# A Fourier mixing layer and a feed-forward block on one core: two transform steps as whole fp32 matmuls, and half of the weights converted ahead of step D

## The chip, the core and the metric

The kernel runs on one core of one Trainium2 chip. The metric is device time in microseconds (us) for one execution, from the first to the last instruction of the core; smaller is better. Of the core's engines, TensorE (PE in the profile, its weight loads PEld), VectorE (DVE), ScalarE (ACT) and GpSimd (POOL) compute. SyncE (SP), ACT and POOL issue DMA transfers, which 16 DMA engines carry.

## The reference

```python
X = np.fft.rfft(x, axis=1)                     # x: (4, 3008, 256)
Xr, Xi = X.real, X.imag
Yr = Xr @ w_r - Xi @ w_i + b_r                 # w_r, w_i: (256, 256)
Yi = Xr @ w_i + Xi @ w_r + b_i
Yr = np.sign(Yr) * np.maximum(np.abs(Yr) - 0.01, 0.0)
Yi = np.sign(Yi) * np.maximum(np.abs(Yi) - 0.01, 0.0)
y = np.fft.irfft(Yr + 1j * Yi, n=3008, axis=1)
h = y.reshape(12032, 256) @ w_in               # w_in: (256, 2048)
g = np.maximum(h, 0.0) + alpha * np.minimum(h, 0.0)
return g @ w_out                               # w_out: (2048, 256)
```

All arrays are fp32.

## The kernel before

The Fourier transform of length 3008 = 47 x 64 is done as two matrix products each way. **Step A** (`a_mm`, L314) multiplies with a table of the 47-point transform, **step B** (`b_mm`) with the 64-point one and the twiddle factors, **step M** (`m_mm`, `m_evac`) mixes the channels and does the soft threshold, **step C** (`c_mm`, L466) and **step D** (`d_step`) go back. Then `l1_step` and `l2_step` are the two products of the feed-forward block. There are 4 batches. In steps A and C the unit of work is a group `g` of two rows (16 for a batch) and a pair `q` of frequency slots (12 for a batch).

Most products split each fp32 operand into two float32r (F32R) parts, `hi` (the upper bits) and `lo` (the rest), and add three matmuls: hi x hi, hi x lo, lo x hi. `split` (L124) makes `hi` by a copy on ACT or DVE and `lo` by a subtraction on DVE or POOL. Steps B and D are different: their operands stay F32, and each `PE.matmul` there is one whole fp32 matmul, which appears in the trace as two records.

The program is written out by hand in one order per engine. What comes before step D of batch 0, the *opening*, is:

1. 36 idle matmuls, then step A of all 16 groups of batch 0 and of the first 4 of batch 1 (`seq`), with splits three groups ahead; 3 idle matmuls follow each of the first 6 groups; then 40 idle matmuls.
2. A loop over `t` in 0 to 12, one pair per turn: `b_mm(t)`, the load for pair t+3, evacuations, `m_mm(t-1)`, `c_mm(t-3)`, and `pump(PT[t])`. A turn's second half waits for the table `rb_s`, of which slots 4 to 11 (pairs 2 to 5) are loaded after step A (`load_rb(4, 12)`).
3. The list `TAIL`, and `a_fill`: the last pairs' steps and the other 12 groups of step A of batch 1. Then step D of the first chunks.

`pump` does the conversion of the feed-forward weights, which arrive as 64-bit words: 16 pieces of 512 KB. A piece takes operations on ACT, four on DVE (`scalar_tensor_tensor` at L247 and three `tensor_scalar`), and three on POOL (L244, L250, L251; for some pieces L250 is on DVE). With one piece in work and the next begun, 4 pumps make a piece: n pieces take 4n + 3 pumps. `CL` (L203) is the number of pieces that are converted in the opening; the rest is pumped in the first 48 steps of the feed-forward block, `PAT[i]` pumps in step i. These 48 steps go in rounds of 6 (two blocks of 128 hidden columns, three chunks each).

`m_evac` (L419) of batch 0 does, on DVE, an add (L424), a clamp (L430) and a subtraction (L435), then ACT makes `Yh` (L440) and DVE `Yl` (L444, `m_evac2`). POOL issues the loads of `bt` (L345), negates two blocks for step M (`b_evac2`, L377) and loads the table `lc_s` of step C (L180).

Of the kernel before, what the change touches and what calls it, by code (L numbers as in the profile page):

```python
# [87 lines left out]

@with_exitstack
def fft_mix_moe(ctx, tc, x, w_r, w_i, b_r, b_i, w_in, w_out, alpha, la, rb, lc, rd, out):  # L90
    nc = tc.nc
# [208 lines left out]

    def a_split(b, g, e=None):
        t = xt[b, g // 2][:, 2 * (g % 2):2 * (g % 2) + 2]
        if b == 1 and g % 2 == 0 and g >= EARLY:
            hl = work.tile([NP, 4, C], F32R, tag="xt", name="xhl")
            hi, lo = hl[:, 0:2], hl[:, 2:4]
        else:
            th, tl = ("Xh", "Xl") if (b == 0 or g < EARLY) and g % 2 else ("xh", "xl")
            hi = work.tile([NP, 2, C], F32R, tag=th, name="xh")
            lo = work.tile([NP, 2, C], F32R, tag=tl, name="xl")
        split(t, hi, lo, e or A, G if g in (LG if b == 0 else LG1) and b < 2 else V)  # L310
# [321 lines left out]

    with tc.manual_schedule():
        nc.gpsimd.dma_start(out=la_s, in_=la)

# [13 lines left out]

        def start_split(n):  # L650
            for b, g in seq[n:n + 1]:
                a_split(b, g, A if g in (HA1 if b else HA) else V)

        for n in range(AHEAD):
            start_split(n)
# [173 lines left out]
```

## Time and profile before

| what | value |
|---|---|
| median of 3 runs (1426.1 to 1431.95) | 1427.29 us |
| the profiled execution, its own time | 1427.34 us |
| its span in the profile | 1425.6 us |
| mean granted TensorE clock | 0.987 of full |
| PE busy | 1387.9 us |
| DVE busy | 831.4 us |
| POOL busy | 440.3 us |

Times in the rows are us from the span's start. A granted clock of 1.00 is 2.4 GHz, 0.50 is 1.2 GHz. A busy PE isn't a PE at its peak: matmuls overlap, so one matmul's record is longer than the time by which it moves the next one on; the text takes that time from the starts.

### The profile page before, as it was taken

To read this page: it belongs to the slowest core of one execution; us is meant where nothing else is said; L and a number is where in the kernel's file an instruction comes from. 1 tells how busy PE (TensorE), PEld (TensorE's weight loads), DVE (VectorE), ACT (ScalarE), POOL (GpSimd) and SP (SyncE) were. 2 spreads that over 40 slices of the span, in tenths; PEclk is the share of its full clock that TensorE was granted. 3 is DMA by queue.
4 is the path that set the end of the run, shared out by engine and by line. 5 is a ranking of instruction groups with operands and counts; after the bars stand their busy time and mean duration, and the time that the engine had idled before them with its cause. 6 is when DMAs were issued, how large, how long until landed. Compare 5 with 4: busy or idle time off the path is not lost.

```text
span 1425.6 us, 25793 instructions
## 1 busy us (share of the span) xinstructions
PE 1387.9 (97%) x9990; PEld 1358.0 (95%) x9990; DVE 831.4 (58%) x1460; ACT 731.4 (51%) x1546; POOL 440.3 (31%) x506
## 2 busy tenths in 40 slices
PE   8979889999999999999999999999999999999998
PEld 5968879999999999999999999999999999999998
DVE  6896886666665444666666454565666444444443
ACT  4435555445445566454454566454544555555554
POOL 5763674222222222222222222222222222222221
PEclk8997999999999999999999999999999999999999
DMA  7954230111011232111110232111101000000000
GB/s 202 228 163 141 74 98 23 58 61 52 27 49 49 61 105 76 44 35 56 53 52 27 63 102 77 36 57 61 56 28 43 30 23 24 23 23 23 23 23 23
DMA packets 62710, 88.21 MB, mean 62 GB/s; under 512 B 10272, under 2 KB 45406, under 8 KB 62588
## 3 DMA queue, kind: packets, MB, share of 16 engines
q1 hardware_dynamic: 54668, 77.02, 18.1%
q0 software_dynamic: 4656, 6.40, 1.8%
q10 hardware_dynamic: 3264, 3.15, 0.6%
q8 instruction: 79, 1.29, 0.4%
q14 instruction: 43, 0.35, 0.1%
HBM read 49.02 MB, written 34.34 MB: 58 GB/s over the span
## 4 chain that ended last, share of the span: by engine, by line
PE 87%; DVE 6%; issue 2%; ACT 2%; DMA 2%; POOL 0%; SPq 0%; DVEq 0%; ACTq 0%; POOLq 0%
PE ps_h L535 35%; PE ps_o L584 8%; PE ps_o L582 8%; PE ps_o L583 8%; PE ps_m L411 5%; PE ps_d L519 4%; PE o_last L584 4%; PE o_last L583 4%; PE o_last L582 4%; PE ps_b L353 2%; PE ps_a L320 1%; PE ps_a L318 1%; PE ps_a L319 1%; DVE q L542 1%; DVE conv L247 1%
## 5 line engine op out<-in xcount | busy, mean ns | idle before, releaser
L535 PE MATMUL ps_h<-yh,w 128*128 128x384 f32 (+1 forms) x1984 | 584.9, 337 | 10.0 <-DVE q L542 10.0
L542 DVE SCALAR_TENSOR_TENSOR q<-q,beta_s,ps_h 128x384 f32<-128x384 f32 (+1 forms) x512 | 309.3, 604 | 346.6 <-ACT q L541 344.2
L547 POOL TENSOR_TENSOR gl<-q,gh 128x384 fp32r<-128x384 f32 (+1 forms) x252 | 257.9, 1023 | 795.8 <-ACT gh L546 678.7
L546 ACT ACTIVATE gh<-q 128x384 fp32r<-128x384 f32 (+1 forms) x512 | 265.8, 519 | 361.1 <-DVE q L542 358.2
L535 PEld LDWEIGHTS ps_h<-yh,w 128*128 128x128 f32 x1984 | 365.5, 188 | 15.3 <-DVE q L542 12.0
L535 PE MATMUL ps_h<-yl,w 128*128 128x384 f32 (+1 forms) x992 | 330.3, 333 | 0.0
L541 ACT ACTIVATE q<-ps_h 128x384 f32<-128x384 f32 (+1 forms) x512 | 245.5, 479 | 157.4 <-PE ps_h L535 140.9
L584 PE MATMUL ps_o<-w,gl 128*128 128x256 f32 x1024 | 289.5, 283 | 0.8 <-POOL gl L547 0.8
L582 PE MATMUL ps_o<-w,gh 128*128 128x256 f32 x1024 | 289.6, 283 | 0.0
L583 PE MATMUL ps_o<-w,gh 128*128 128x256 f32 x1024 | 285.1, 278 | 0.0
L547 DVE TENSOR_TENSOR gl<-q,gh 128x384 fp32r<-128x384 f32 (+1 forms) x260 | 157.0, 604 | 100.3 <-ACT gh L546 99.3
L584 PEld LDWEIGHTS ps_o<-w,gl 128*128 128x128 f32 x1024 | 192.9, 188 | 1.2 <-POOL gl L547 1.2
L583 PEld LDWEIGHTS ps_o<-w,gh 128*128 128x128 f32 x1024 | 192.8, 188 | 0.0
L582 PEld LDWEIGHTS ps_o<-w,gh 128*128 128x128 f32 x1024 | 192.7, 188 | 0.0
L535 PEld LDWEIGHTS ps_h<-yl,w 128*128 128x128 f32 x992 | 188.0, 190 | 1.3
L584 PE MATMUL o_last<-w,gl 128*128 128x256 f32 x480 | 135.3, 282 | 0.0
L583 PE MATMUL o_last<-w,gh 128*128 128x256 f32 x480 | 134.7, 281 | 0.0
L582 PE MATMUL o_last<-w,gh 128*128 128x256 f32 x480 | 134.2, 280 | 0.0
L584 PEld LDWEIGHTS o_last<-w,gl 128*128 128x128 f32 x480 | 90.7, 189 | 0.0
L582 PEld LDWEIGHTS o_last<-w,gh 128*128 128x128 f32 x480 | 90.3, 188 | 0.0
L583 PEld LDWEIGHTS o_last<-w,gh 128*128 128x128 f32 x480 | 90.2, 188 | 0.0
L519 PE MATMUL ps_d<-rd_s,zt 96*128 96x128 f32 x512 | 64.4, 281 | 0.0
(120 smaller groups left out, 1664.5 us busy)
## 6 DMA issues: line engine op xcount, KB each, us to landing
zt<-zd SPq DMA_DIRECT2D x32, 384.0 KB
ad<-ast SPq DMA_DIRECT2D x48, 192.0 KB
bt<-ad SPq DMA_DIRECT2D x72, 128.0 KB
zd<-zst SPq DMA_DIRECT2D x36, 256.0 KB
xt<-in_x SPq DMA_DIRECT2D x18, 320.0 KB
out<-os SPq DMA_DIRECT2D x34, 128.0 KB
x<-in_x SPq DMA_DIRECT2D x13, 320.0 KB
raw<-in_moe_w_in SPq DMA_DIRECT2D x8, 512.0 KB
```

Source lines behind the costliest of these rows:

```text
L247: lambda: V.scalar_tensor_tensor(out=v1, in0=wh, scalar=0xC0000000, in1=v1, op0=ALU.bitwise_and, op1=ALU.bitwise_or),
L353: PE.matmul(ps[:, s, ct], t[:, s, 128 * ct:128 * ct + 128], rb_s[:, 2 * q + s], start=True, stop=True)
L411: PE.matmul(p, a[:, k:k + 128], mix[i][:, w, ct], start=(n == 0), stop=(n == 3 * CT - 1))
L519: PE.matmul(ps[:, i], t[:, i, 128 * ct:128 * ct + 128], rd_s, start=True, stop=True)
L535: PE.matmul(ps, wi_h[m // FH][:, w, ct, 128 * (m % FH):128 * (m % FH) + 128], a[:, ct, 0:n], start=(k == 0), stop=(k == 3 * CT - 1))
L541: A.activation(out=q, in_=ps, func=AF.Relu, scale=-1.0)
L542: V.scalar_tensor_tensor(out=q, in0=q, scalar=beta_s[:, m:m + 1], in1=ps, op0=ALU.mult, op1=ALU.add)
L546: A.activation(out=hi, in_=q, func=AF.Copy)
L547: (V if LOS[(2 * m + c) % len(LOS)] and fill or not fill and (m + c) % 2 else G).tensor_tensor(out=lo, in0=q, in1=f(hi), op=ALU.subtract)
L582: PE.matmul(a, hi[:, t], w[:, 0], start=(i, k) in first, stop=False)
L583: PE.matmul(a, hi[:, t], w[:, 1], start=False, stop=False)
L584: PE.matmul(a, lo[:, t], w[:, 0], start=False, stop=(i, k) in last)
```

## The change

Step A of batches 0 and 1 takes `x` and a table `lf_s` in F32, one whole matmul for a group instead of three F32R ones, and its splits are gone, with the idle matmuls between the groups. In batch 0 DVE evacuates every second group. Step C of batch 0 takes the thresholded `Y` in F32 and a table `cf_s`: two whole matmuls for a pair instead of six, no `Yh` and no `Yl`. `cf_s` (half the bytes of `lc_s`) stands in the place of `lc_s`, which is loaded in step 26 of the feed-forward block, for batch 1. `CL` is 8, so 8 of 16 pieces are converted in the opening, and `PT` has 32 pumps instead of 19, with 3 left for `TAIL`. `PAT` is as it was.

```diff
@@ tables
+    cf_s = const.tile([128, NSLOT, 128], F32, tag="lc", name="cf_s")
+    def load_cf(n0, n1):
+        nc.gpsimd.dma_start(out=cf_s[:, n0:n1], in_=cf[:, n0:n1])
+    def load_lc():
+        lc_s = const.tile([128, 2, NSLOT, 128], F32R, tag="lc", name="lc_s")
...
+        for n in range(0, NSLOT, 6):
+            nc.gpsimd.dma_start(out=lc_s[:, :, n:n + 6], in_=lc[:, :, n:n + 6])
@@
-    CL = 4
+    CL = 8
@@ a_mm
+        if b < 2:
+            PE.matmul(ps, lf_s, xt[b, g // 2][:, 2 * (g % 2):2 * (g % 2) + 2], start=True, stop=True)
+            return
         hi, lo = xp.pop((b, g))
         PE.matmul(ps, la_s[:, 0], hi, start=True, stop=False)
         PE.matmul(ps, la_s[:, 1], hi, start=False, stop=False)
         PE.matmul(ps, la_s[:, 0], lo, start=False, stop=True)
@@ a_evac
-        A.activation(out=st, in_=ps, func=AF.Copy)
+        if b == 0 and g % 2:
+            V.tensor_copy(out=st, in_=ps)
+        else:
+            A.activation(out=st, in_=ps, func=AF.Copy)
@@ m_evac
-        m_less(b, q, t, c)
-        m_evac1(b, q)
+        y = work.tile([128, 2, C], F32, tag="Yh", name="Y")
+        V.tensor_tensor(out=y, in0=t, in1=c, op=ALU.subtract)
+        ys[b, q] = y
@@ c_mm
+        if b == 0:
+            y = ys.pop((b, q))
+            for s in range(2):
+                PE.matmul(ps[:, s], cf_s[:, 2 * q + s], y[:, s], start=True, stop=True)
+            return
@@
-    PT = [0, 0, 1, 2, 3, 2, 2, 1, 2, 3, 1, 2]
-    TAIL = [['s', 1, 1], ['p', 99], ['ce', 3], ['me', 1], ['s', 2, 0], ['cm', 2], ['m2', 1], ['f', 2], ['cm', 1], ['f', 0], ['ce', 2], ['ce', 1], ['f', 4]]
+    PT = [1, 2, 3, 3, 3, 3, 3, 3, 3, 3, 3, 2]
+    TAIL = [['ce', 3], ['me', 1], ['cm', 2], ['p', 99], ['f', 1], ['ce', 2], ['cm', 1], ['f', 1], ['ce', 1], ['f', 3]]
@@ opening
             a_mm(b, g)
-            if n < 6:
-                keep_warm(3)
@@ loop over t
-            run(m_evac2, t - 2)
-                load_lc(3 * t, 3 * t + 6)
+                load_cf(3 * t, 3 * t + 6)
-            if 9 <= t:
-                for g in range(2 * t - 18, 2 * t - 16):
-                    if EARLY // 2 <= g:
-                        a_load(1, g)
+            if 8 <= t < 11:
+                for g in range(2 * t - 14, 2 * t - 12):
+                    a_load(1, g)
@@ feed-forward block
+        at(LM, load_lc)
```

On **PE** the end of the opening (`TAIL` and `a_fill`) stands so before: the last step C in threes, then step A of batch 1 in threes, each third on a `lo` part (`xhl` and `xh`, `xl` are split parts of x).

```order
L473 MATMUL ps_c<-Yh,lc_s 128x256
L474 MATMUL ps_c<-Yh,lc_s 128x256
L475 MATMUL ps_c<-Yl,lc_s 128x256
L318 MATMUL ps_a<-xhl,la_s 96x512
L319 MATMUL ps_a<-xhl,la_s 96x512
L320 MATMUL ps_a<-xhl,la_s 96x512
L318 MATMUL ps_a<-xh,la_s 96x512
L319 MATMUL ps_a<-xh,la_s 96x512
L320 MATMUL ps_a<-xl,la_s 96x512
```

In the changed kernel (its own line numbers) the same place, up to step D:

```order
L486 MATMUL ps_c<-Y,cf_s 128x256 x4
L324 MATMUL ps_a<-x_292,lf_s 96x512
L486 MATMUL ps_c<-Y,cf_s 128x256 x2
L324 MATMUL ps_a<-x_292,lf_s 96x512 x11
L537 MATMUL ps_d<-rd_s,zt 128x128 x16
```

One group stands between the last two pairs of step C, and eleven groups follow without anything between them; before, two groups stood there and ten followed.

On **POOL** two turns of the loop (load of `bt`, the two negations, then conversion of a piece, `w` and `conv`) stand so before:

```order
L345 DMA bt<-a_82 128x1x256 x2
L377 TENSOR_SCALAR Xh<-Xh 128x4x64
L377 TENSOR_SCALAR Xl<-Xl 128x4x64
L244 TENSOR_TENSOR conv<-conv 128x512
L180 DMA lc_s<-tab_lc 128x2x768
L345 DMA bt<-a_82 128x1x256 x2
L377 TENSOR_SCALAR Xh<-Xh 128x4x64
L377 TENSOR_SCALAR Xl<-Xl 128x4x64
L250 TENSOR_TENSOR conv<-conv,w_385 128x512
L251 TENSOR_TENSOR w_385<-conv 128x2x256
```

and now:

```order
L356 DMA bt<-a_83 128x1x256 x2
L388 TENSOR_SCALAR Xh<-Xh 128x4x64
L388 TENSOR_SCALAR Xl<-Xl 128x4x64
L253 TENSOR_TENSOR conv<-conv 128x512
L259 TENSOR_TENSOR conv<-conv,w_243 128x512
L260 TENSOR_TENSOR w_243<-conv 128x2x256
L356 DMA bt<-a_83 128x1x256 x2
L388 TENSOR_SCALAR Xh<-Xh 128x4x64
L388 TENSOR_SCALAR Xl<-Xl 128x4x64
L253 TENSOR_TENSOR conv<-conv 128x512
```

A whole piece stands behind one pair, and the next piece begins behind the next.

On **DVE** one turn of the loop (threshold of one pair, `Xl` of another, conversion) stands so before:

```order
L424 TENSOR_TENSOR Yt<-ps_m,bias 128x512
L430 TENSOR_SCALAR Yc<-Yt 128x512
L435 TENSOR_TENSOR Yt<-Yt,Yc 128x512
L373 TENSOR_TENSOR Xl<-ps_b,Xh 128x4x128
L444 TENSOR_TENSOR Yl<-Yt,Yh 128x512
L235 TENSOR_SCALAR conv<-conv 128x512
L247 SCALAR_TENSOR_TENSOR conv<-raw,conv 128x512
```

and now:

```order
L435 TENSOR_TENSOR Yt<-ps_m,bias 128x512
L442 TENSOR_SCALAR Yc<-Yt 128x512
L438 TENSOR_TENSOR Y<-Yt,Yc 128x512
L384 TENSOR_TENSOR Xl<-ps_b,Xh 128x4x128
L244 TENSOR_SCALAR conv<-conv 128x512
L256 SCALAR_TENSOR_TENSOR conv<-raw,conv 128x512
L238 TENSOR_SCALAR conv<-conv 128x512
```

`Yl` is gone from the turn, and one more conversion operation stands in it.

## Rows read from the trace of the kernel before

**Rows 1.** The page's first part: busy us of each engine, share, instructions.
```profile
PE 1387.9 (97%) x9990; PEld 1358.0 (95%) x9990; DVE 831.4 (58%) x1460; ACT 731.4 (51%) x1546; POOL 440.3 (31%) x506
```
**Rows 2.** Busy by stretch: PE, PEld, DVE, ACT, POOL, granted clock, DMA share, GB/s.
```profile
57.00:98.00 41.00, 34.98 (x280) 33.31 (x278) 39.74 (x49) 16.04 (x28) 30.55 (x37) 1.00 0.71 204
105.70:118.36 12.66, 12.66 (x32) 8.33 (x31) 8.83 (x12) 6.98 (x12) 3.89 (x3) 0.50 0.74 232
```
**Rows 3.** PE in order of time, 0 to 45 us: start, us, instruction, idle time before.
```profile
4.84 0.71 PE L318 MATMUL ps_a<-xh,la_s 94*96 94x512 f32 x1
...
30.80 3.98 PE L631 MATMUL ps_idle<-idle 128*128 128x128 bf16 x40
...
42.10 1.13 PE L353 MATMUL ps_b<-rb_s,bt 128*128 128x128 f32 x8 [0.96 <-DMA rb_s<-tab_rb]
```
**Rows 4.** Stretches of step A, columns as in rows 2.
```profile
17.00:20.40 3.40, 2.65 (x11) 1.22 (x9) 3.30 (x5) 2.20 (x5) 1.80 (x3) 1.00 1.02 215
20.40:23.90 3.50, 2.22 (x9) 1.05 (x7) 3.40 (x4) 2.51 (x5) 2.74 (x2) 0.99 1.06 348
...
27.30:30.70 3.40, 3.40 (x9) 1.97 (x7) 1.44 (x1) 1.92 (x4) 3.40 (x5) 0.50 0.38 101
```
**Rows 5.** The chain that ended last, in order of time: start, us, what.
```profile
32.10 9.86 DMA rb_s<-tab_rb
...
118.57 3.43 PE ps_d L519 x16
```
**Rows 6.** DVE in order of time, in the loop and at its end.
```profile
71.07 2.83 DVE L444 TENSOR_TENSOR Yl<-Yt,Yh 128x512 fp32r<-128x512 f32 x1
...
75.97 0.43 DVE L430 TENSOR_SCALAR Yc<-Yt 128x512 f32<-128x512 f32 x1
76.43 0.69 DVE L435 TENSOR_TENSOR Yt<-Yt,Yc 128x512 f32<-128x512 f32 x1
...
77.82 0.93 DVE L444 TENSOR_TENSOR Yl<-Yt,Yh 128x512 fp32r<-128x512 f32 x1
78.68 0.68 DVE L247 SCALAR_TENSOR_TENSOR conv<-raw,conv 128x512 uint32<-128x512 uint32 x1
...
83.44 0.41 DVE L235 TENSOR_SCALAR conv<-conv 128x512 uint32<-128x512 uint32 x1
...
97.62 1.63 DVE L435 TENSOR_TENSOR Yt<-Yt,Yc 128x512 f32<-128x512 f32 x1
```
**Rows 7.** POOL in order of time, in the loop.
```profile
71.31 0.42 POOL L377 TENSOR_SCALAR Xh<-Xh 128x256 fp32r<-128x256 f32 x1
...
72.06 1.28 POOL L250 TENSOR_TENSOR conv<-conv,w 128x512 f32<-128x512 f32 x1
...
95.94 1.35 POOL L251 TENSOR_TENSOR w<-conv 128x512 fp32r<-128x512 f32 x1
```
**Rows 8.** Waits of PE, 122 to 240 us: us in total, times, longest.
```profile
PE ps_h L535 <- DVE q L542: 14.6, 20, 1.3
```
**Rows 9.** Rounds of 6 feed-forward steps, columns as in rows 2.
```profile
139.54:156.41 16.87, 13.33 (x90) 12.10 (x89) 15.66 (x21) 9.18 (x19) 11.65 (x9) 1.00 0.20 63
...
199.63:216.11 16.48, 11.85 (x77) 10.84 (x78) 15.22 (x20) 8.84 (x19) 11.97 (x9) 1.00 0.22 72
216.11:228.72 12.61, 11.31 (x84) 11.11 (x83) 10.46 (x17) 6.53 (x15) 8.30 (x7) 1.00 0.01 2
228.72:241.49 12.77, 12.77 (x96) 12.77 (x96) 6.78 (x15) 6.91 (x17) 3.66 (x5) 1.00 0.04 14
```
**Rows 10.** PE in order of time around step D (L519).
```profile
118.36 5.88 PE L519 MATMUL ps_d<-rd_s,zt 96*128 96x128 f32 x32
...
127.69 1.95 PE L519 MATMUL ps_d<-rd_s,zt 96*128 96x128 f32 x16
129.40 0.42 PE L535 MATMUL ps_h<-yh,w 128*128 128x384 f32 x1
```
**Rows 11.** POOL in order of time, in step A: the load of batch 1's x lands.
```profile
17.78 1.27 POOL L131 TENSOR_TENSOR xl<-x,xh 94x512 fp32r<-94x512 f32 x1 [0.50 <-DMA xt<-in_x]
```

More of the change, by code (lines that the diff above doesn't have):

```diff
@@ L84, in dft_tables, with fft_mix_moe @@
     f = np.float32
-    return (two_parts(la.astype(f)), rb.reshape(128, NSLOT, 128).astype(f),
-            two_parts(lc.reshape(128, NSLOT, 128).astype(f)), rd.astype(f))
+    la, lc = la.astype(f), lc.reshape(128, NSLOT, 128).astype(f)
+    return two_parts(la), rb.reshape(128, NSLOT, 128).astype(f), two_parts(lc), rd.astype(f), la, lc
 @with_exitstack
-def fft_mix_moe(ctx, tc, x, w_r, w_i, b_r, b_i, w_in, w_out, alpha, la, rb, lc, rd, out):
+def fft_mix_moe(ctx, tc, x, w_r, w_i, b_r, b_i, w_in, w_out, alpha, la, rb, lc, rd, lf, cf, out):
     nc = tc.nc
@@ L134, in fft_mix_moe @@
     la_s = const.tile([NP, 2, NQ], F32R, name="la_s")
+    lf_s = const.tile([NP, NQ], F32, name="lf_s")
     rb_s = const.tile([128, NSLOT, 128], F32, name="rb_s")
-    lc_s = const.tile([128, 2, NSLOT, 128], F32R, name="lc_s")
+    cf_s = const.tile([128, NSLOT, 128], F32, tag="lc", name="cf_s")
+    lc_h = []
     rd_s = const.tile([NQ, 128], F32, name="rd_s")
@@ L177, in load_rb @@
         nc.sync.dma_start(out=rb_s[:, n0:n1], in_=rb[:, n0:n1])
-    def load_lc(n0, n1):
-        nc.gpsimd.dma_start(out=lc_s[:, :, n0:n1], in_=lc[:, :, n0:n1])
+    def load_cf(n0, n1):
+        nc.gpsimd.dma_start(out=cf_s[:, n0:n1], in_=cf[:, n0:n1])
+    def load_lc():
+        lc_s = const.tile([128, 2, NSLOT, 128], F32R, tag="lc", name="lc_s")
+        lc_h.append(lc_s)
+        for n in range(0, NSLOT, 6):
+            nc.gpsimd.dma_start(out=lc_s[:, :, n:n + 6], in_=lc[:, :, n:n + 6])
     def split_mix():
@@ L299, in fft_mix_moe, with a_split @@
     xp = {}
-    def a_split(b, g, e=None):
+    def a_split(b, g):
         t = xt[b, g // 2][:, 2 * (g % 2):2 * (g % 2) + 2]
[L303 to L310, printed above, removed]
+        hi = work.tile([NP, 2, C], F32R, tag="xh", name="xh")
+        lo = work.tile([NP, 2, C], F32R, tag="xl", name="xl")
+        split(t, hi, lo, A, V)
         xp[b, g] = hi, lo
@@ L315, in a_mm @@
     def a_mm(b, g):
+        ps = ps_f.tile([NQ, 2, C], F32, tag="f", name="ps_a")
+        pa[b, g] = ps
+        if b < 2:
+            PE.matmul(ps, lf_s, xt[b, g // 2][:, 2 * (g % 2):2 * (g % 2) + 2], start=True, stop=True)
+            return
         hi, lo = xp.pop((b, g))
-        ps = ps_f.tile([NQ, 2, C], F32, tag="f", name="ps_a")
         PE.matmul(ps, la_s[:, 0], hi, start=True, stop=False)
@@ L320, in a_mm @@
         PE.matmul(ps, la_s[:, 0], lo, start=False, stop=True)
-        pa[b, g] = ps
     def a_evac(b, g):
@@ L468, in c_mm @@
             zd[b] = dram.tile([NQ, R, C], F32, tag="zd", name=f"zd{b}")
+        ps = ps_f.tile([128, 2, C], F32, tag="f", name="ps_c")
+        pc[b, q] = ps
+        if b == 0:
[3 more added lines that the diff above has]
+            return
         hi, lo, _ = ys.pop((b, q))
-        ps = ps_f.tile([128, 2, C], F32, tag="f", name="ps_c")
+        lc_s, = lc_h
         for s in range(2):
@@ L475, in c_mm @@
             PE.matmul(ps[:, s], lc_s[:, 0, k], lo[:, s], start=False, stop=True)
-        pc[b, q] = ps
     def c_evac(b, q):
@@ L633, in fft_mix_moe @@
     with tc.manual_schedule():
+        nc.gpsimd.dma_start(out=lf_s, in_=lf)
         nc.gpsimd.dma_start(out=la_s, in_=la)
@@ L648, in fft_mix_moe @@
         seq = [(0, g) for g in range(NG)] + [(1, g) for g in range(EARLY)]
[L650 to L655, printed above, removed]
         for n, (b, g) in enumerate(seq):
-            start_split(n + AHEAD)
             a_mm(b, g)
-            if n < 6:
-                keep_warm(3)
             if n >= 1:
@@ L682, in a_fill @@
             for g in range(a1[0], min(a1[0] + n, NG)):
-                if g + 3 < NG:
-                    a_split(1, g + 3, A if SE[(g + 3) % len(SE)] else V)
                 a_mm(1, g)
@@ L690, in fft_mix_moe @@
         for t in range(NPAIR + 1):
-            for g, e in AT.get(t, ()):
-                a_split(1, EARLY + g, A if e else V)
             run(b_mm, t)
@@ L706, in fft_mix_moe @@
             if t < 8 and t % 2 == 0:
-                load_lc(3 * t, 3 * t + 6)
-            if 9 <= t:
-                for g in range(2 * t - 18, 2 * t - 16):
-                    if EARLY // 2 <= g:
-                        a_load(1, g)
+                load_cf(3 * t, 3 * t + 6)
+            if 8 <= t < 11:
+                for g in range(2 * t - 14, 2 * t - 12):
+                    a_load(1, g)
         for op, *args in TAIL:
-            if op == "s":
-                a_split(1, EARLY + args[0], A if args[1] else V)
-            elif op == "f":
+            if op == "f":
                 a_fill(*args)
@@ L719, in fft_mix_moe @@
             else:
-                {"me": m_evac, "m2": m_evac2, "cm": c_mm, "ce": c_evac}[op](0, NPAIR - args[0])
+                {"me": m_evac, "cm": c_mm, "ce": c_evac}[op](0, NPAIR - args[0])
         put()
@@ L820 @@
         add(f"in_{name}", a)
-    for name, a in zip(("la", "rb", "lc", "rd"), dft_tables()):
+    for name, a in zip(("la", "rb", "lc", "rd", "lf", "cf"), dft_tables()):
         add(f"tab_{name}", a)
```

8 lines of the change are left out of this document (removed).

## The prediction

> **What bounds the kernel now.** I read the page's busy times first, then the busy times by stretch, then each stretch in order of time. PE is busy 1387.9 us of a span of 1425.6 [rows 1], so after the opening only work taken from PE, or idle time of PE, can bring anything. The opening (up to 124 us) and the first rounds of the feed-forward block (up to 229 us) are another matter.
>
> *Step A* begins on PE at 4.84 us and its last matmul makes way for the 40 idle ones at 30.80 [rows 3]. DVE is busy 3.30 of 3.40 us in its middle, with splits, while the granted clock is 1.00; PE then has gaps (2.22 of 3.50 us busy), and from the next row on the clock is 0.50, with PE busy without a gap [rows 4].
>
> *The gate of the loop* is a transfer: slots 4 to 11 of `rb_s` are asked for at 32.10, when step A has ended, and land 9.86 us later [rows 5]; `b_mm` of pair 2 starts at 42.10 behind it [rows 3].
>
> *The loop* ends for DVE with the last `m_evac`, at 97.62 + 1.63 = 99.25 [rows 6]: 57.2 us from the gate. DVE looks full (39.74 of 41.00 us, POOL 30.55) [rows 2], but much of it is waiting inside instructions. `Yl` takes 0.93 us at 77.82 and 2.83 us at 71.07 [rows 6]; the long one ends when POOL's row of 71.31 to 73.34 has run out [rows 6, 7]. So DVE operations that work from SBUF alone and POOL's tensor operations take turns. I call that the *shared turn* and add their undisturbed times:
>
> - a threshold: 0.43 + 0.69; a `Yl`: 0.93; a pair's two negations: 2 x 0.41 or 0.42 (0.82);
> - a piece: on DVE 0.68 + 3 x 0.41, on POOL 2 x 1.28 + 1.35, together 5.8 [rows 6, 7].
>
> From the gate on these are 12 thresholds (13.4), 11 `Yl` (10.2), 10 pairs of negations (8.2) and 4 pieces (23.3): 55.1 us, against 57.2 measured. The turn is taken all the time, and a stretch is 1.04 times the sum.
>
> *The end of the opening* runs from 99.25 to step D at 118.36 [rows 10], 19.1 us; for 12.66 us of it PE does step A of batch 1 without a gap at clock 0.50 [rows 2].
>
> *The first rounds*: PE waits 14.6 us for DVE's `q` [rows 8], which stands behind conversions. A round without conversion is 12.77 us less one step D, 1.71 from start to start [rows 9, 10]: 11.06. The six rounds from 139.54 to 228.72 take 89.2 [rows 9]; they hold 45 pumps (from the 7th to the 51st and last).
>
> **The change, part by part.** Durations are of one profiled execution, 1427.34 us by its own time, practically the median of the runs (1427.29).
>
> *A whole fp32 matmul.* Step D's are such: 16 records of 128 columns take 1.71 us from start to start at clock 1.00 (127.69 to 129.40) and 3.43 us at 0.50 [rows 10, 5], so 0.107 or 0.214 for 128 columns of one record. A group of step A has 512 columns and two records: 0.86 us at 2.4 GHz, 1.72 at 1.2.
>
> *Step A of the opening.* All splits go, and PE waits for x alone. The last x (batch 1's) has landed by 17.78 [rows 11]. I let two groups run at 1.2 GHz and 18 at 2.4: 4.84 + 3.44 + 15.5 = 23.8 instead of 30.8, **-7.0**. The gate follows its stores, so it moves by as much, to 35.1. The evacuations on ACT and DVE are shorter than a group. Both ends: 20 groups at 1.2 GHz give 39.2 (+8.4), all at 2.4 give 22.0 (-8.8).
>
> Which clock? At 1.00 PE kept it while it was busy 2.65 of 3.40 us with the same 94x96 operands, and lost it with 2.22 of 3.50 [rows 4]; now it has no gaps. At 0.50, though, step A without a gap didn't bring it back in 12.66 us [rows 2]; step D's whole fp32 matmuls did: 32 of them take 5.88 us, of which 16 took 3.43 [rows 10, 5]. I take 2.4 GHz, since stage and loop reach these groups at full clock. The Trainium skill (page "TensorE: Matmul & The Clock Gate", section "What's actually happening") says that the throttled clock is the default and that activity of TensorE releases it. By that rule groups without gaps come out at the sum below; the 12.66 us speak against it, and by them the first two rivals hold.
>
> *The loop.* `Yl` goes; the conversion grows from 19 to 32 pumps, of which 3 come before the gate; 29 / 4 = 7.25 pieces are 42.2 us. With thresholds (13.4) and negations (8.2) the sum is 63.8, times 1.04 is 66.2: **+9.0**. PE's share, with two whole matmuls of 256 columns (0.86 us) a pair for six split ones, stays covered: it was busy 34.98 of 41 us [rows 2] and the pairs now come more slowly. The tables are half as large, the raw pieces 2 MB more; the DMA share was 0.71 [rows 2]. In SP's queue the second load of `rb_s` (pairs 6 to 8) now stands behind a raw piece that waits for DVE in turn 2; with four turns until it is needed I cost that at nothing, and the loads of batch 1's x, moved forward to turns 8 to 10, too: no raw piece comes behind them before the block. Ends: nothing above the plain sum (-2.4), or DVE's PSUM operations, two of 0.68 us a pair by the same 512-element pattern as L247's row [rows 6], no longer hidden beside POOL in ten pairs (+13.6).
>
> *The end of the opening.* Behind the last threshold PE has two matmuls of step C (0.86), then 11 groups (9.5), which wait for no split; with 0.6 us for the handover 11.0 us instead of 19.1: **-8.1**. Three pumps are left over; they go to DVE, POOL and ACT beside these groups. `zt` is loaded meanwhile; SP has five stores ahead of it instead of six. At 1.2 GHz it is 20.4 (+1.3).
>
> *The first step D*: 32 records at 0.107 are 3.4 us instead of 5.6 (5.88 less the 0.3 by which the last record outlasts its turn): **-2.2**. With the clock down nothing is saved.
>
> *The first rounds.* 16 of the 51 pumps go. The six rounds exceed 6 x 11.06 = 66.4 by 22.8 us, 0.51 for a pump; some of it belongs to the combining of the mixing weights, which stays, so 0.45: **-7.2**. `PAT` gives 36 pumps by step 28, so the rounds 199.63 to 216.11 and 216.11 to 228.72 lose nearly all of theirs. The four loads of `lc_s` in step 26 stand in POOL's queue ahead of one conversion and the `gl` splits; two chunks wait in `gh` and `gl` (4 buffers each), so I cost them at nothing. Ends: 0, or 16 x 0.51 and the two rounds at 11.06 (-10).
>
> Sum: -7.0 + 9.0 - 8.1 - 2.2 - 7.2 = -15.5; 1427.3 - 15.5 = **1412 us**.
>
> **The rivals.**
>
> 1. *The clock is down at the end of the opening only.* For: the same place was at 0.50 before [rows 2]. Against: no gap now leads into it. Eleven groups cost 0.86 more (9.4) and step D's gain goes (2.2): 1423 us.
> 2. *Slower: the whole fp32 groups run at 1.2 GHz in both places.* Each costs 0.86 us more than I count. Eighteen more in the first stage (15.4) and rival 1's 11.6 make 1439 us. From 18 such groups on the change is a loss. For: the long stretch at 0.50 without a gap [rows 2, 4]. Against: step D's fp32 matmuls raised the clock [rows 10].
> 3. *The shared turn isn't filled so well*, since POOL's queue and DVE's now wait on each other for every piece, and the PSUM operations come on top: +13.6, 1425 us. For: POOL gets 1.6 times its work there. Against: the factor of 1.04 before.
> 4. *The first rounds don't shorten*, because `gl` splits fill the freed turn: +7.2, 1419 us. Against: the 11.06 us of the round without conversion.
>
> **How the numbers follow.** A measurement of this kernel can tell 0.5% (7.1 us) from no change. The forecast has 0.56, rival 4 0.10 (both faster by more than that), rival 1 0.12, rival 3 0.11 (both within it), rival 2 0.11 (slower). So 0.66 faster, 0.23 same, 0.11 slower. The range: down to 1403 (the loop at its plain sum, the rounds at -10, step A all at 2.4 GHz), up to 1426, which takes in rivals 1, 3 and 4 and leaves out rival 2 and a little at the bottom.
>
> **What would show it.** The idle matmuls behind step A begin near 24 us and the second `b_mm` stretch near 35; the last threshold ends near 101; step A of batch 1 is spaced by 0.86 us, with clock 1.00, and step D begins near 112; the rounds without conversion are two more than before, near 11 us each. A spacing of 1.72 us with clock 0.50 in step A, a last threshold after 110, or rounds that stay at 15 us would prove the forecast wrong.

## The result, and the profile after

| | median | runs | ratio to before, 95% interval |
|---|---|---|---|
| before | 1428.09 us | 4, 1426.1 to 1431.95 | |
| changed | 1413.49 us | 4, 1411.02 to 1415.04 | 0.9893 [0.9866, 0.9919] |

The change makes the kernel about 1% faster: the forecast was 1412 us. The profiled execution of the changed kernel took 1414.38 us by its own time, 13.0 less than that of before. The page's first part, which answers to [rows 1]:

```profile
PE 1381.0 (98%) x9916; PEld 1345.5 (95%) x9916; DVE 787.8 (56%) x1413; ACT 716.7 (51%) x1519; POOL 423.8 (30%) x497
```

PE is busy 6.9 us less by this row; the other 6 us are idle time that PE no longer has. Where they went stands in the order of time. PE of the changed kernel (start, us, instruction, idle time before it), to be read against [rows 3, 10]:

```profile
24.21 1.10 PE L324 MATMUL ps_a<-xt,lf_s 94*96 94x512 f32 x2 [1.43 <-ACT ast L342]
25.15 2.40 PE L641 MATMUL ps_idle<-idle 128*128 128x128 bf16 x40
...
36.56 1.13 PE L364 MATMUL ps_b<-rb_s,bt 128*128 128x128 f32 x8 [1.94 <-DMA rb_s<-tab_rb]
...
41.89 1.06 PE L364 MATMUL ps_b<-rb_s,bt 128*128 128x128 f32 x8
...
102.11 9.67 PE L324 MATMUL ps_a<-x,lf_s 94*96 94x512 f32 x22
112.36 3.90 PE L537 MATMUL ps_d<-rd_s,zt 96*128 96x128 f32 x32 [0.58 <-DMA zt<-zd]
```

Step A ends at 25.15 instead of 30.80, the gate (pair 2) opens at 36.56 instead of 42.10, and step D begins at 112.36 instead of 118.36. The 22 records before step D are 11 whole groups in 9.67 us, 0.87 apart: full clock. The granted clock by stretch, in step A, behind the gate and in that place (columns as in [rows 2]):

```profile
4.00:8.00 4.00, 4.00 (x15) 2.02 (x13) 0.21 (x1) 0.59 (x1) 0.00 (x0) 1.00 0.99 254
...
36.00:40.00 4.00, 3.44 (x20) 3.47 (x21) 2.12 (x4) 1.94 (x4) 1.99 (x3) 0.70 1.07 153
40.00:44.00 4.00, 4.00 (x32) 4.00 (x32) 2.69 (x6) 1.03 (x2) 3.15 (x6) 0.87 1.01 144
...
108.00:112.00 4.00, 3.78 (x9) 1.14 (x7) 0.00 (x0) 2.73 (x6) 0.00 (x0) 1.00 0.97 261
```

At the start of step A the row of the clock doesn't hold. The first group's records (count; duration in ns: least, median, most; first and last start) are

```profile
L324 PE MATMUL ps_a<-x,lf_s x2: 1061/1088/1114, 4.8 to 5.7; 94*96 94x512 f32 x2
```

and the median of step A's records is 592. So the first group, and part of the second, still ran at 1.2 GHz; from 7.2 us on the records of 592 ns show 2.4 GHz.

Behind PE's wait of 1.94 us at the gate the clock falls to 0.70 and 0.87, in PE-bound work: b_mm of the next pair comes 5.33 us behind the gate (3.77 to 3.84 in runs below where the clock held).

In the loop, the chain of waits (start, us, what) runs through the conversion: on POOL first, whose loads of `bt` stand behind it, then on DVE:

```profile
53.23 1.43 POOL conv L253
54.66 1.69 POOL conv L259
56.44 1.32 POOL w L260
58.33 1.37 POOL bt L356 x2
...
79.21 1.65 DVE conv L256
81.49 0.80 DVE Yc L442
```

Four of the seven rounds of the feed-forward block that answer to [rows 9], from the 7th step to the 49th:

```profile
132.51:147.60 15.09, 12.54 (x86) 11.52 (x85) 13.88 (x21) 8.59 (x19) 9.07 (x8) 1.00 0.23 69
...
175.55:190.46 14.91, 10.78 (x78) 10.38 (x77) 9.93 (x14) 5.74 (x13) 13.72 (x13) 1.00 0.33 101
190.46:203.45 12.99, 12.99 (x87) 12.99 (x87) 7.52 (x13) 6.82 (x14) 5.13 (x5) 0.87 0.36 129
203.45:214.77 11.32, 11.32 (x86) 11.32 (x85) 5.86 (x13) 5.67 (x12) 1.01 (x1) 1.00 0.00 0
```

They take 96.05 us in all (132.51 to 228.56), against 101.95 before. PE's wait for `q` halved, and another grew from 0.8 us before (118 to 242 us), both in the waits from 112 to 229 us (total, times, longest):

```profile
PE ps_h L553 <- DVE q L560: 7.1, 9, 1.5
PE ps_o L602 <- POOL gl L565: 5.3, 4, 2.6
```

All stages of the profiled executions, this one's and those of the experiments below, stand in one table. "Loop" is from the gate to the end of the last threshold (pair 11), "end" from there to step D, "first steps" from step D to DVE's 7th `q`, "rounds" from the 7th to the 49th; what follows is 1184 us in each (1183.8 to 1184.4).

| kernel | gate at | loop | end | first steps | rounds | span |
|---|---|---|---|---|---|---|
| before | 42.10 | 60.70 | 15.56 | 21.18 | 101.95 | 1425.6 |
| changed | 36.56 | 64.46 | 11.34 | 20.15 | 96.05 | 1412.6 |
| a_only | 36.81 | 58.99 | 12.71 | 21.23 | 101.26 | 1415.3 |
| c_only | 45.42 | 52.75 | 13.06 | 21.11 | 102.04 | 1418.2 |
| b_cl8 | 44.75 | 74.24 | 15.36 | 19.55 | 91.76 | 1429.7 |
| cl4 | 36.27 | 50.51 | 11.27 | 20.65 | 102.10 | 1404.8 |
| lc_late | 34.50 | 63.13 | 11.96 | 20.99 | 91.74 | 1406.7 |
| cl5_tail | 37.26 | 52.91 | 11.73 | 20.34 | 100.64 | 1406.9 |
| best | 36.60 | 50.86 | 11.65 | 22.75 | 99.83 | 1406.0 |
| best_warm | 36.76 | 50.82 | 11.45 | 21.01 | 99.90 | 1404.2 |
| no_warm | 48.41 | 62.99 | 11.27 | 19.76 | 96.06 | 1422.5 |

### The profile page after: what moved, and what is told of

It reads as the page before. It is cut to its first block, busy times and chain, and to the rows that moved or that the text cites. A ratio compares the mean times of both kernels' runs of the same rounds, so it can differ in the third digit from the quotient of the medians.

```text
span 1412.6 us, 25487 instructions
## 1 busy us (share of the span) xinstructions
PE 1381.0 (98%) x9916; PEld 1345.5 (95%) x9916; DVE 787.8 (56%) x1413; ACT 716.7 (51%) x1519; POOL 423.8 (30%) x497
## 4 chain that ended last, share of the span: by engine, by line
PE 87%; DVE 3%; POOL 3%; DMA 3%; issue 2%; ACT 1%; SPq 1%; ACTq 0%; DVEq 0%; POOLq 0%
PE ps_h L553 35%; PE ps_o L602 8%; PE ps_o L600 8%; PE ps_o L601 8%; PE ps_m L422 5%; PE o_last L602 4%; PE o_last L601 4%; PE o_last L600 4%; PE ps_d L537 4%; PE ps_b L364 2%; DMA x<-in_x 1%; DVE conv L256 1%; PE ps_m L408 1%; DVE q L560 1%; DMA raw<-in_moe_w_in 1%
## 5 line engine op out<-in xcount | busy, mean ns | idle before, releaser
L565 DVE TENSOR_TENSOR gl<-q,gh 128x384 fp32r<-128x384 f32 (+1 forms) x260 | 152.3, 586 | 103.9 <-ACT gh L564 101.8
```

Source lines behind the costliest of these rows:

```text
L565: (V if LOS[(2 * m + c) % len(LOS)] and fill or not fill and (m + c) % 2 else G).tensor_tensor(out=lo, in0=q, in1=f(hi), op=ALU.subtract)
```

## The experiments

The theory to be tested: the whole fp32 steps are the gain, and converting four more pieces ahead takes back part of it, since in the loop DVE and POOL share the turn in which the pieces are made. The rival: the work moved ahead is what pays.

### The parts apart

**The whole fp32 steps without the moved pieces** (cl4):

```diff
-    CL = 8
+    CL = 4
-    PT = [1, 2, 3, 3, 3, 3, 3, 3, 3, 3, 3, 2]
+    PT = [0, 0, 1, 2, 3, 2, 2, 1, 2, 3, 1, 2]
```

> The changed kernel with CL = 4 and the PT of before: 19 pumps in the opening instead of 35, the two transform steps stay whole fp32. Theory (shared turn): the four pieces that are put back into the first feed-forward rounds cost about 5.9 us there (the six rounds from 132.51 to 228.56 took 96.05, those of before 101.95) and took 5.8 us each of the turn of DVE and POOL in the loop. Without them PE bounds the loop at 46 to 49 us from the gate instead of 64.5, step D begins near 97 instead of 112.4, the rounds take near 102: 1404 us, between 1400 and 1408. Rival (converting ahead is what pays): the rounds give back more than the loop wins, 1420 us or more. Rival (the loop is bound by something else, such as DVE's PSUM operations or the transfers): the loop stays above 58 us and the time at 1411 to 1418.

Measured: 1406.56 us (5 runs, 1405.36 to 1408.11), ratio to before 0.9849 [0.9828, 0.987]. This lies in the theory's range (1400 to 1408), and both rivals fall. Its loop as one stretch, and PE's rows there:

```profile
36.27:86.78 50.51, 50.51 (x389) 49.08 (x390) 43.04 (x62) 18.90 (x32) 38.29 (x49) 1.00 0.72 202
```

```profile
40.11 1.08 PE L364 MATMUL ps_b<-rb_s,bt 128*128 128x128 f32 x8
44.75 1.05 PE L364 MATMUL ps_b<-rb_s,bt 128*128 128x128 f32 x8
49.38 1.05 PE L364 MATMUL ps_b<-rb_s,bt 128*128 128x128 f32 x8
```

PE is busy in all 50.51 us, 4.63 us a pair: the loop is PE's own. The changed kernel's loop is 13.95 us longer by the four pieces, and its rounds 6.05 shorter.

**The moved pieces without the whole fp32 steps** (b_cl8: the kernel before, with)

```diff
-    CL = 4
+    CL = 8
-    PT = [0, 0, 1, 2, 3, 2, 2, 1, 2, 3, 1, 2]
+    PT = [1, 2, 3, 3, 3, 3, 3, 3, 3, 3, 3, 2]
-    TAIL = [['s', 1, 1], ['p', 99], ['ce', 3], ['me', 1], ['s', 2, 0], ['cm', 2], ['m2', 1], ['f', 2], ['cm', 1], ['f', 0], ['ce', 2], ['ce', 1], ['f', 4]]
+    TAIL = [['p', 99], ['s', 1, 1], ['ce', 3], ['me', 1], ['s', 2, 0], ['cm', 2], ['m2', 1], ['f', 2], ['cm', 1], ['f', 0], ['ce', 2], ['ce', 1], ['f', 4]]
```

> The kernel before with the second part of the change alone: CL = 8, the PT of the changed kernel, and the remaining pumps first in TAIL; steps A and C stay split. Theory (shared turn): thresholds 13.4, Yl 10.2, negations 8.2 and 7.25 pieces 42.2 us sum to 74.0, times 1.04 is 77 us for the loop against 57.2, and the six feed-forward rounds give back 6 to 7: about 1441 us, between 1435 and 1448. Rival (converting ahead pays by itself): 1420 us or less.

Measured: 1432.97 us (12 runs, 1429.84 to 1435.94), ratio 1.0034 [1.0022, 1.0047]: slower than before, as the theory has it, though by less than its range (1435 to 1448). The loop grew by 13.54 us (60.70 to 74.24) and the rounds gave back 10.19, where 6 to 7 were forecast. The gate came 2.65 us later, which is not from the edit: step A ahead of it is the same program, but in this execution it ended at 33.82 instead of 30.80, with a clock of 0.50 from 10 us on against a mean of 0.75 before. Two of its rounds:

```profile
196.95:209.61 12.66, 11.43 (x85) 11.23 (x84) 8.97 (x13) 5.63 (x13) 11.07 (x9) 1.00 0.02 6
209.61:221.12 11.51, 11.51 (x88) 11.51 (x87) 7.27 (x14) 6.26 (x14) 4.63 (x4) 1.00 0.00 1
```

The same two rounds of the changed kernel took 14.91 and 12.99. This kernel loads `lc_s` in its opening; the changed one does so in step 26, in the first of the two. That led to lc_late below.

**Step A alone as whole fp32** (a_only; the kernel before, with)

```diff
+        if b < 2:
+            pa[b, g] = ps
+            PE.matmul(ps, lf_s, xt[b, g // 2][:, 2 * (g % 2):2 * (g % 2) + 2], start=True, stop=True)
+            return
...
-            if n < 6:
-                keep_warm(3)
```

> The kernel before with step A of batches 0 and 1 alone as whole fp32 matmuls; step C stays split and CL is 4. Theory: the gate of the loop comes 5.5 us earlier, the end of the opening (last threshold to step D) takes 11 to 12 us instead of 19.1 at a granted clock of 1.00, the first step D takes 2 us less, the loop stays at 57 us and the rounds at 102: -15 us, 1412 us, between 1409 and 1416. Rival (the clock at the end of the opening needs the whole fp32 matmuls of step C as well): it stays at 0.50 there, groups of step A 1.72 us apart, 1423 us.

Measured: 1416.46 us (6 runs, 1415.76 to 1417.72), ratio 0.9917 [0.9901, 0.9934], just above the expected range (1409 to 1416). The groups at the end of the opening ran at full clock (20 records in 8.75 us), so the rival falls. But PE then waited 1.93 us for `zt`, and the clock fell in step D, whose 32 records took 7.07 us instead of the changed kernel's 3.90. In order of time:

```profile
97.83 8.75 PE L315 MATMUL ps_a<-x,lf_s 94*96 94x512 f32 x20
108.51 7.07 PE L522 MATMUL ps_d<-rd_s,zt 96*128 96x128 f32 x32 [1.93 <-DMA zt<-zd]
```

**Step C alone as whole fp32** (c_only; the kernel before, with)

```diff
-        m_less(b, q, t, c)
-        m_evac1(b, q)
+        y = work.tile([128, 2, C], F32, tag="Yh", name="Y")
+        V.tensor_tensor(out=y, in0=t, in1=c, op=ALU.subtract)
+        ys[b, q] = y
```

and `c_mm`, `load_cf` and `load_lc` as in the change.

> The kernel before with step C of batch 0 alone as whole fp32 matmuls (no Yh, no Yl; lc_s loaded in the feed-forward block); step A stays split and CL is 4. Theory: Yl (10.2 us of the shared turn) goes, PE bounds the loop at 48 to 50 us instead of 57.2; step A of batch 1 keeps its splits and its clock of 0.50, so the end of the opening stays near 19 us: about -8, 1419 us, between 1416 and 1423. Rival (the last step C as whole fp32 raises the clock for what follows): the end of the opening takes 12 to 14 us and the time is 1412 to 1414. Rival (Yl was hidden in waits): 1426 to 1429.

Measured: 1418.5 us (6 runs, 1415.52 to 1420.09), ratio 0.9928 [0.9909, 0.9947]: in the theory's range. The loop fell from 60.70 to 52.75 us. Of those 52.75 some 1.4 are again a clock that fell behind the gate, after a wait of 2.90 us: the next b_mm came 5.21 us later. Two things that the theory didn't have nearly cancel in this execution. The gate came 3.32 us later, as its split step A ran at 0.50 and ended at 33.69. And the end took 13.06 us instead of 15.56, since the clock stayed up for longer than before, where it is 0.50 from 105.70 on, 2.9 us behind the last threshold [rows 2]:

```profile
98.17:106.40 8.23, 6.55 (x25) 3.42 (x24) 8.06 (x11) 4.92 (x10) 5.56 (x4) 1.00 0.69 220
106.40:111.23 4.83, 4.83 (x13) 2.92 (x12) 2.69 (x6) 3.12 (x6) 0.00 (x0) 0.50 0.94 293
```

The second rival named such an end, 12 to 14 us. But the clock did fall again in it, and step C can't have raised a clock that was full already; why it stayed up for longer is open.

By the medians of this set of runs (before 1428.77) step A brings 12.3 us, step C 10.3, and both together 22.2 (cl4). The parts add up. The moved pieces cost 4.2 on the kernel before, and 6.9 on the whole fp32 steps (1413.49 against 1406.56; the first is from the set of the result, where before took 1428.09).

### Whether two engines share a turn

The theory's turn was read from pairs of long rows. This run has neither transform nor block, only DVE and POOL operations on 128x512 tiles:

```diff
+    for kind in ("two", "one", "psum"):
+        stage(kind, 12, 0)
+    stage("two", 0, 12)
+    for kind, nv in (("two", 24), ("one", 40), ("psum", 24)):
+        stage(kind, nv, 12)
```

> No transform and no feed-forward block: the output is zeros. In separate stages DVE does 128x512 fp32 operations by themselves (tensor_tensor from SBUF, tensor_scalar from SBUF, tensor_tensor with one operand from PSUM), POOL does tensor_tensor by itself, and then each kind of DVE operation runs beside 12 of POOL's. Theory (shared turn): alone 0.69, 0.43, 0.68 and 1.28 us as in the loop; beside POOL, 24 two-operand DVE operations (16.6) and 12 of POOL's (15.4) take about 32 us, 40 tensor_scalar (17) and 12 of POOL's also about 32, but the 24 from PSUM overlap and take 17 to 20. Rival (no turn is shared, the long Yl rows were something else): all three stages take 16 to 18 us.

Measured, in order of time: DVE alone with two operands from SBUF, with one, and with one from PSUM; POOL alone; then POOL beside each of the three.

```profile
22.94 8.69 DVE L120 TENSOR_TENSOR vo<-va,vb 128x512 f32<-128x512 f32 x12
...
34.74 4.57 DVE L122 TENSOR_SCALAR vo<-va 128x512 f32<-128x512 f32 x10
...
42.20 8.67 DVE L124 TENSOR_TENSOR vo<-ps,vb 128x512 f32<-128x512 f32 x12
...
53.07 16.50 POOL L126 TENSOR_TENSOR go<-ga,gb 128x512 f32<-128x512 f32 x12
...
71.72 20.11 POOL L126 TENSOR_TENSOR go<-ga,gb 128x512 f32<-128x512 f32 x12
72.40 28.70 DVE L120 TENSOR_TENSOR vo<-va,vb 128x512 f32<-128x512 f32 x24
...
103.55 16.99 POOL L126 TENSOR_TENSOR go<-ga,gb 128x512 f32<-128x512 f32 x12
...
105.34 27.94 DVE L122 TENSOR_SCALAR vo<-va 128x512 f32<-128x512 f32 x38
...
135.50 16.55 POOL L126 TENSOR_TENSOR go<-ga,gb 128x512 f32<-128x512 f32 x12
136.18 17.37 DVE L124 TENSOR_TENSOR vo<-ps,vb 128x512 f32<-128x512 f32 x24
```

Beside POOL, 24 two-operand operations take 28.70 us instead of 17.4 (twice 8.69), 38 of one operand 27.94 instead of 17.4; with an operand in PSUM DVE is as fast as alone. So the turn is shared, and only by operations from SBUF: the rival falls. The Trainium skill (page "GPSIMD Engine Reference", section "Specifications") says that GpSimd's SBUF interfaces are shared with VectorE, for two SBUF inputs or a two-port mode. The rows of two operands and of PSUM agree; in which mode the operations of one operand ran, no run shows.

But the times don't add up as the theory has it (32 us). Records from the stretch of two operands in which both engines work, and of POOL alone:

```profile
L120 DVE TENSOR_TENSOR vo<-va,vb x11: 1632/1633/1636, 72.4 to 89.1; 128x512 f32<-128x512 f32 x11
L126 POOL TENSOR_TENSOR go<-ga,gb x10: 1588/1590/1591, 73.6 to 88.6; 128x512 f32<-128x512 f32 x10
L126 POOL TENSOR_TENSOR go<-ga,gb x11: 1259/1262/1262, 54.9 to 68.3; 128x512 f32<-128x512 f32 x11
```

The two engines start operations alternately, one and one, each 1.67 us apart (72.4 to 89.1 in ten steps). Alone, DVE's are 0.73 apart and POOL's 1.34. So a pair of operations takes 1.67 us where the sum is 2.07, a factor of 0.81; with one operand it takes 1.40 of 1.80, a factor of 0.78.

### The wait that the change brings

`lc_s` later (lc_late; the changed kernel, with)

```diff
-        for n in range(0, NSLOT, 6):
-            nc.gpsimd.dma_start(out=lc_s[:, :, n:n + 6], in_=lc[:, :, n:n + 6])
+        for k in range(4):
+            at(42 + 2 * k, load_lc_part, 6 * k)
```

> The changed kernel with the four loads of lc_s one each in steps 42, 44, 46 and 48 of the feed-forward block instead of all in step 26. Theory (the four issues hold up POOL's queue for 2.94 us, and the third term of ps_o waits 2.6 us for a gl behind them): the rounds from the 7th step to the 49th take 93 to 94 us instead of 96.05, the time is 1411 us, between 1410 and 1412. Rival (another gl split is late there all the same, as in the kernel before with CL = 8 alone, which loads lc_s in the opening and has one wait of 2.0 us for gl): within 1 us of 1413.5.

Measured: 1408.8 us (5 runs, 1406.55 to 1409.65), ratio 0.9867 [0.9844, 0.9891]. The theory's sign, and more than its size: the rounds take 91.74 us, 4.3 less, as b_cl8's did. The changed kernel's POOL around the loads with PE's wait behind it, then two of lc_late's rounds:

```profile
182.94 1.61 POOL L259 TENSOR_TENSOR conv<-conv,w 128x512 f32<-128x512 f32 x1
184.50 2.94 POOL L189 DMA_DIRECT2D lc_s<-tab_lc  x4
187.47 1.27 POOL L260 TENSOR_TENSOR w<-conv 128x512 fp32r<-128x512 f32 x1
188.69 2.29 POOL L565 TENSOR_TENSOR gl<-q,gh 128x384 fp32r<-128x384 f32 x2
190.06 0.38 PE L602 MATMUL ps_o<-w,gl 128*128 128x256 f32 x1 [2.58 <-POOL gl L565]
```

```profile
173.63:186.27 12.64, 11.13 (x83) 10.93 (x82) 8.95 (x14) 5.63 (x13) 11.05 (x9) 1.00 0.01 4
186.27:197.77 11.50, 11.50 (x88) 11.50 (x87) 7.26 (x13) 6.27 (x14) 4.64 (x4) 1.00 0.01 1
```

The loads take 2.94 us of POOL's queue, PE waits 2.58 us for the `gl` behind them, and the next round then runs at a clock of 0.87, which makes it 12.99 us instead of 11.50. The two rounds give 2.27 and 1.49 of the 4.3 us, the one after them 0.56 (10.76 instead of 11.32). Of the rest of this run's gain, 2.06 us are an earlier gate, behind which the clock held; that comes ahead of the edit and is not from it. The intervals of the two kernels' ratios overlap; what carries the verdict is the rounds, the same to 0.02 us in pairs of executions (96.05 and no_warm's 96.06 with the loads in step 26, 91.74 and b_cl8's 91.76 without them).

### The clock

No idle matmuls at the start (no_warm; the changed kernel, with)

```diff
-        keep_warm(36)
+        keep_warm(1)
```

> The changed kernel with one idle matmul at the start instead of 36. Theory (whole fp32 matmuls raise the clock themselves): the first groups of step A are 1.72 us apart, the granted clock then goes to 1.00, and step A ends 3 to 7 us later than at 25.15, so the time is 1416 to 1421 us. Rival (the clock in step A is only kept, not raised, by these groups): it stays at 0.50, step A ends near 40 and the time is 1427 us or more. Rival (the clock does not depend on it): the time stays within 3 us of 1413.5.

Measured: 1424.12 us (10 runs, 1422.33 to 1424.94), ratio 0.9971 [0.9958, 0.9985]: between theory and rival. The records of step A's 16 groups of batch 0 (duration in ns: least, median, most; first and last start), of no_warm and of the changed kernel:

```profile
L324 PE MATMUL ps_a<-x,lf_s x32: 1061/1061/1169, 4.3 to 30.8; 94*96 94x512 f32 x32
```

```profile
L324 PE MATMUL ps_a<-x,lf_s x32: 592/592/1114, 4.8 to 19.3; 94*96 94x512 f32 x32
```

All 20 groups ran at 1.2 GHz, from 4.29 to 38.53 us, without a gap. So the rival's mechanism holds: these groups didn't raise the clock in 34 us. In the changed kernel it rose near 7 us, 2 us behind the 36 idle matmuls, and the groups kept it. The price is the gate, 11.85 us later. The Trainium skill (page "TensorE: Matmul & The Clock Gate", section "What's actually happening") has activity release the throttle; for these groups no run here shows that.

The same with the table of step A padded with zeros from 96 to 128 columns (no_warm_wide):

```diff
-    lf_s = const.tile([NP, NQ], F32, name="lf_s")
+    lf_s = const.tile([NP, 128], F32, name="lf_s")
...
+            ps = ps_f.tile([128, 2, C], F32, tag="f", name="ps_a")
+            pa[b, g] = ps[0:NQ]
```

> The run no_warm (one idle matmul at the start) with the table of step A padded with zeros from 96 to 128 columns, so that the same groups are 94x128 and every group counts 512 columns as before; the padded part of the result is not used. Theory (it is the width of the table: step D's 96x128 matmuls and the 128x128 idle ones raised the clock in other runs, the 94x96 ones, whole or split, did not): the groups come down from 1.72 to 0.86 us apart within step A and step A ends before 30 us instead of 38.5. Rival (the width does not matter): all 20 groups stay 1.7 us apart and step A ends near 38.

Measured: one run, 1423.88 us, step A from 4.79 to 39.08. The rival: the width is not it. What raised the clock in step D [rows 10] and not here stays open.

### A version that is faster

**A fifth piece, its second half in TAIL between the groups** (cl5_tail; cl4, with CL = 5 and)

```diff
-    TAIL = [['ce', 3], ['me', 1], ['cm', 2], ['p', 99], ['f', 1], ['ce', 2], ['cm', 1], ['f', 1], ['ce', 1], ['f', 3]]
+    TAIL = [['ce', 3], ['me', 1], ['cm', 2], ['p', 1], ['f', 1], ['ce', 2], ['cm', 1], ['f', 1], ['ce', 1], ['f', 1], ['p', 1], ['f', 1], ['p', 99], ['f', 1]]
```

> The kernel cl4 (whole fp32 steps, CL = 4, PT of before) with a fifth piece whose second half, four pumps, stands in TAIL between the groups of step A of batch 1, where DVE waited 12.8 us and POOL 18.0. Theory: the opening stays PE's (step D within 0.5 us of 98.05) and the rounds win a quarter of what four pieces brought (6.05 us): 1.5 us, so 1405 us. Rival (ACT, which copies each group out of PSUM, is held up by the conversion and step D begins later): step D 1 to 3 us later, 1406 to 1409 us.

Measured: 1406.1 us (4 runs, 1405.36 to 1408.63), ratio 0.9854 [0.983, 0.9878]: the same as cl4. The rounds won 1.46 us, as forecast. Step D came 3.85 later in the profiled execution, for a reason that neither side named: PE waited 4.04 us at the gate and the clock fell behind it (the next b_mm 6.25 us later). One execution can't say whether this goes with the edit.

**The same with the late loads of `lc_s`** (best; cl5_tail, with)

```diff
+        for k in range(4):
+            at(42 + 2 * k, load_lc_part, 6 * k)
```

> The kernel cl5_tail with the loads of lc_s in steps 42 to 48. Theory: with fewer pieces in front of POOL the four loads cost less than with CL = 8, where they cost 4.3 us: the rounds go from 100.6 to between 97 and 100, the time to 1403 to 1406 us. Rival (with CL = 4 or 5 POOL's queue is late anyway, since the kernels before and cl4, without and with the loads, have the same rounds of 102): no change, 1406 us.

Measured: 1406.35 us (5 runs, 1405.16 to 1407.82), ratio 0.984 [0.9821, 0.9859]: by the time, the rival. The rounds went from 100.64 to 99.83, the upper edge of the theory's 97 to 100. In the profiled execution the first steps hid this: they took 2.41 us more than cl5_tail's, as PE waited 2.27 us for `q` at 108.9 and the clock was 0.69 from 112 to 116.

**And with 24 idle matmuls at the gate** (best_warm; best, with)

```diff
+            if t == 2:
+                keep_warm(24)
             run(b_mm, t)
```

> The kernel best with 24 more idle matmuls between the mixing of pair 0 and step B of pair 2, in the time in which PE waits for the rest of rb_s. Theory: the clock no longer falls behind that wait (it fell to 0.70 in 36 to 44 us of the changed kernel, and b_mm of the next pair came 5.33 us later there against 3.77 to 3.84 where it held): 0 to 2 us less than best. Rival (the wait is short in most executions and the idle matmuls are in the way): 0 to 1 us more than best.

Measured: 1405.71 us (4 runs, 1405.09 to 1407.15), ratio 0.984 [0.982, 0.9859]. No difference to best that these runs can tell; the clock held behind the gate in both profiled executions, so the run didn't try its own point.

Four versions with 4 or 5 pieces lie within 1 us, 0.5% below the changed kernel. cl4 is the simplest of them.

## Why the prediction was right

The time was right, 1412 against 1413.49 us, and so was most of its working: what the whole fp32 groups bring, the full clock, and that the loop gets longer. That the sum came within 1.5 us is in part luck, since several terms were mis-sized and their errors cancel. The terms, against the profiled executions:

| step | forecast | measured |
|---|---|---|
| step A and the gate | -7.0 | -5.54 |
| loop and end of the opening together | +0.9 | -0.46 |
| first step D | -2.2 | -1.97 (3.66 us up to the first matmul of the block, 5.63 before) |
| the other first steps | 0 | +0.95 |
| rounds | -7.2 | -5.90 |
| all that follows | 0 | -0.03 |
| sum | -15.5 | -12.96 |

- **Step A and the gate.** The prediction let two of the 20 groups run at 1.2 GHz; one did, and part of the second. Step A still ended at 25.15, not 23.8. PE stood for 1.43 us ahead of the last group: the copy that frees its PSUM buffer was in ACT's queue behind the split of the mixing weights, for whose transfers ACT waited 2.30 and 0.42 us. The transfer of the gate was asked for only at 29.66, behind four stores in SP's queue, 4.5 us after the end of step A instead of 1.3, but took 6.77 us instead of 9.86. So the gate moved as far as step A (-5.54 and -5.65), the forecast's rule, by two changes that cancel.

- **The loop.** The prediction read the row at 97.62 [rows 6] as the last threshold. It is the last of the loop, pair 10's; pair 11's stands in TAIL, in order of time on DVE of before:

```profile
102.11 0.69 DVE L435 TENSOR_TENSOR Yt<-Yt,Yc 128x512 f32<-128x512 f32 x1
```

  So 12 thresholds ended at 102.80, 60.70 us from the gate and not 57.2, and the end took 15.56 and not 19.1. The wrong endpoint cancels in the sum. The factor doesn't: 60.70 over the 55.1 of the sum is 1.10, not 1.04, and with it the loop would have come out at 70.3 us, 4 more than forecast. Measured were 64.46, 1.01 of the sum of 63.8.

- **The shared turn.** That DVE's operations from SBUF and POOL's share something was right. That their times add up was not: a pair takes 1.67 us where the sum is 2.07 (turn). Against the prediction's sum the loops of before, the changed kernel and b_cl8 (eight pieces less two operations, 77.6 us) took 1.10, 1.01 and 0.96: each further piece costs less than its 5.8 us. From before to b_cl8 the loop grew by 13.54 us for nearly four pieces, some 3.5 a piece. From cl4 to the changed kernel it grew by 13.95 for 3.25, 4.3 a piece, which is no clean price, since cl4's loop is PE's. That the changed loop came out at 1.01 of the plain sum is luck: other waits in it made up for the overlap. DVE was busy only 54.0 of the 64.46 us, ACT waited 15.7 for POOL's `w` and 5.4 for a raw piece.

- **The clock.** Full clock in both places was right, and rivals 1 and 2 didn't come. The reason given against rival 2, that step D's fp32 matmuls raised the clock, is no reason for step A: no_warm's groups didn't raise it. What holds for the end of the opening is the other reason, that the loop reaches these groups at full clock; in step A it rose near 7 us, behind the idle matmuls.

- **The end and step D.** From the last threshold to step D 11.0 were forecast and 11.34 measured. The 0.6 us of handover in it, which no row gave, were 0.15 ahead of step C and 0.58 of waiting for `zt`. The first step D was 0.2 off its number.

- **The rounds.** The step that failed is "so I cost them at nothing", of the four loads of `lc_s`. They cost 4.3 us (lc_late): `gl` came late behind them on POOL, PE waited 2.58 us for it, and the clock fell. Without them the 16 moved pumps bring 10.2 us, 0.64 a pump, the far end of that term (-10) and not its 0.45. So two errors, of 3.0 and 4.3 us, made the term look right. (The forecast is of six rounds, which took 6.9 us less; the seventh, without conversion, took 1.02 more, with 105 records of PE between the same two `q` instead of 96, so all seven are compared.) Rival 4 named the tile `gl`, but as one that fills DVE's freed turn; the rounds did shorten, and its lateness came from the loads.

- **The first steps** grew by 0.95 us: the next raw piece lands only at 120.03 (5.26 us from 114.77), and ACT waits 1.92 us for it. The prediction had no term there; no run tried whether this is the whole cause.

- **The range.** Its lower bound, 1403, is not what its own ends give: -2.4 in the loop, -2.8 in the rounds and -1.8 in step A make 1404.8.

## What to carry to other kernels

A stage may be moved ahead of another only into time that nobody there needs: four pieces cost 13.95 us in the loop and gave back 6.05 to 10.2, and only because the whole fp32 steps had made more room did the change as a whole pay. Try the parts apart, since a gain of 22 us hid a loss of 7. And cost every DMA issue by the queue in which it stands, even where its data are needed much later; what it costs hangs on what waits behind it, as the same four loads cost 4.3 us with eight pieces converted and 0.8 with five.

## What the runs showed of the hardware that was not expected

- DVE and POOL operations of 128x512 that work from SBUF were started alternately while both engines had work: 1.67 us apart on each for DVE's of two operands (0.73 alone), 1.40 for those of one (0.46 alone), against 1.34 of POOL's alone. So beside a busy POOL an operation of one operand was nearly as dear to DVE as one of two. With an operand from PSUM DVE's stayed at 0.73 and POOL's at 1.34.
- Gapless groups of step A, whole fp32 on 94 rows, stayed at 1.2 GHz for 34 us, 96 or 128 columns wide; the same groups held 2.4 GHz in the changed kernel from 7 us on.
- In no_warm the row of the granted clock reads 1.00 from 0 to 44 us although each record of step A takes 1061 ns instead of 592, and so it does over the first group of the changed kernel. At the start of a trace the durations, not the clock row, tell the clock.
- Short waits of PE can cost twice. Waits of 1.94, 1.93 and 2.58 us (at the gate, before a_only's step D, in the rounds) were each followed by a clock of 0.57 to 0.87 in the work behind them. With 0.58 us before the changed kernel's step D it held, and with 2.27 us at best's gate too, but behind another wait of 2.27 us in best's first steps it fell.
- Step A as three split matmuls a group ended at 30.80, 33.69 and 33.82 us in three executions of the same program part (before, c_only, b_cl8), with a clock of 0.50 for most of it in the last two.
